# Attention beside a gelu MLP on one core: which side work may go on in a step of the main loop, finer steps, and a chunk's scaling moved ahead

## The chip, the core and the metric

The kernel runs on one core of a Trainium2 chip. The core has five engines that matter here: TensorE (PE in the profile, its weight loads PEld) multiplies matrices into PSUM, VectorE (DVE) and ScalarE (ACT) work element by element, GpSimd (POOL) does a little set-up, and SyncE (SP) issues most DMA transfers. Each engine takes its instructions strictly in the order in which the program lists them and waits where one needs another engine's result. The metric is the device time of one execution in microseconds; the figure given is the median of several executions.

## What is computed

The input has 2048 tokens of width 640. After a layer norm without weights, two branches are added to the input: multi-head attention with 32 heads of width 20, and a second layer norm with a two-layer MLP of width 1536 and tanh-approximated gelu. All arrays are float32.

```python
xn = _layernorm(x, axis=-1)
return x + _A_ref(xn, A_wqkv, A_wo) + _B_ref(xn, B_w1, B_b1, B_w2, B_b2)

# _A_ref: 32 heads of width 20
scores = jnp.einsum("bhqd,bhkd->bhqk", q, k) * (Dh ** -0.5)
p = _softmax(scores, axis=-1)
o = jnp.einsum("bhqk,bhkd->bhqd", p, v)
return o.transpose(0, 2, 1, 3).reshape(B, S, D) @ wo

# _B_ref
y = _layernorm(x, axis=-1)
h = _gelu(jnp.einsum("bsd,df->bsf", y, w1) + b1)
return jnp.einsum("bsf,fd->bsd", h, w2) + b2
```

## The kernel before

**Stages.** From 0 to about 232 us the kernel normalises x, splits the weights into pairs of 16-bit numbers and computes q, k and v; q and k, and the normalised x, go out to DRAM. From 232 to about 1308 us runs the attention loop, into which the MLP is woven. After that only the output projection is left (lines 872 to 904), which runs to 1377 us on TensorE, with the last output store behind it.

**The attention loop.** The heads are taken in 16 pairs `g` and two halves `hf` of the queries (`ORDER`, line 37): the first twelve pairs take both halves in turn, the last four take all first halves and then all second halves. One `(g, hf)` has two column blocks `cc` of 512 queries and 16 blocks `kb` of 128 keys. A *unit* is one `kb` of both heads: two score matmuls into a PSUM tile `s` of which there are three (line 584), and one exponential on ScalarE over 128 x 1024 (line 586). Four units are a *group*; there are 256 groups. For the first two units of each group VectorE computes `low`, what the upper 16 bits of `p` leave (line 598). `pv` (lines 603 to 638) multiplies a group's `p` and `low` with the values into the PSUM tile `o`; it is issued one group late, so that the product of group n follows the scores of group n + 1.

**The order written by hand** stands in lines 933 to 962. For each group it is: scores of units 0 and 1, a `tick()`, `low` of unit 0, a slice of *fill*, scores of units 2 and 3, a `tick()`, `low` of unit 1, and the product of the previous group. So there are two ticks in a group.

**Fill** is the generator `chain()`: the MLP's matmuls, then the output projection. Each group gives it a credit of 1.235 us (`rate`), and its yields book the cost of the matmuls issued: 0.3276 us for three matmuls of the first layer (`pu`, line 787), 0.272 us for two of the second (`py`, line 819), 0.408 us for three of the projection (`z`, line 896). A slice ends when the credit or `CHUNK` is used up, or when a PSUM tile has been completed (`over`). The MLP goes through eight chunks of 256 tokens (`MC`). Within a chunk six first-layer tiles alternate with four second-layer tiles of the chunk before; at the border between two chunks three first-layer tiles follow one another with one second-layer tile among them. There is one PSUM tile `m` (pool `psM`, one buffer) for `pu`, `py` and `z` alike, so a new tile's matmuls wait until VectorE has read the last.

**Side work** is a list of generators, `sides`; every tick takes each of them one step further (lines 520 to 530). They are:

- `gelu` (lines 735 to 753), one for each first-layer tile, begun when its matmuls are done: two vector instructions that read the tile, at the next tick two more, a tick later nothing, then the tanh on ScalarE, then three vector instructions. The first tile of a chunk also scales the chunk's row factors `r2f` (line 739).
- `addup` (lines 755 to 762), one vector instruction for each second-layer tile, and the store and next load of the running sum at the second of two.
- `load_stack` (lines 131 to 152): the DMAs that bring the next pair's q and k.
- `finish` (lines 666 to 733), the heads' normalisation, run one after another by `finishing()`. After pairs 3, 6, 9, 12, 14 and 16 (`ENDS`), for each half, the outputs and the sums of the exponentials come back from DRAM; VectorE adds, checks and inverts the sums (lines 702 to 707, the small group); the inverse goes through DRAM to be spread over rows; then, for each of two column blocks, four vector instructions add, scale and split the outputs (lines 725 to 731, each in a tick of its own), and a DMA stores them to `oscr`. The very last one is timed by the counts `W1` and `W2` in ticks after the loop.
- `prep_late` (lines 534 to 558): once the last chunk's first layer is done, wo is loaded into the room of w1, its squares are summed on ScalarE (line 541), a matmul adds the sums over partitions (line 110), and VectorE splits wo (lines 552 to 557).

The chunk's x and row factors are loaded by `load_chunk` (lines 769 to 775) about one chunk ahead. `projection()` starts a piece only when its heads are finished (`known`, line 873).

Of the kernel before, what the change touches and what calls it, by code (L numbers as in the profile page):

```python
# [12 lines left out]
ALU = mybir.AluOpType  # L13
# [29 lines left out]
def mha_mlp_kernel(tc, x, wqkv, wo, w1, b1, w2, b2, out):  # L43
# [4 lines left out]
    with (  # L48
# [463 lines left out]
        with ExitStack() as scope:  # L512
# [7 lines left out]
            sides = []  # L520

            def begin(it):

                if next(it, self_end) is not self_end:
                    sides.append(it)

            def tick():
                for it in list(sides):
                    if next(it, self_end) is self_end:
                        sides.remove(it)  # L530

            self_end = object()

            def prep_late(tag, w, wv_, src, nk, slices, delay):
                nc.sync.dma_start(w, src)
                for _ in range(delay):
                    yield
                acc = sm.tile([P, 8], F32, tag="acc", name="acc")
                for i, sl in enumerate(slices):
                    junk = m1.tile([P, 2 * MC], F32, tag="u", name="junk").bitcast(BF16)[:, :D]  # L540
                    nc.scalar.activation(junk, w[:, sl, :], AF.Square, accum_out=acc[:, i : i + 1])
                    yield
                pw[tag] = pow2(acc[:, : len(slices)], tag)
                s = keep.tile([P, 1], F32, name=f"s_{tag}")
                nc.vector.tensor_scalar(s, pw[tag][1], 4096.0, None, ALU.mult)
                nc.vector.tensor_scalar(fo, pw["v"][0], 2.0**-22, pw[tag][0], ALU.mult, ALU.mult)
                yield
                for k in range(nk):
                    parts = []
                    for tag_, c0 in (("u", 0), ("w", 320)):  # L550
                        tmp = m1.tile([P, 2 * MC], F32, tag=tag_, name="wtmp")[:, :320]
                        nc.vector.tensor_scalar(tmp, w[:, k, c0 : c0 + 320], s, None, ALU.mult)
                        parts.append((tmp, slice(c0, c0 + 320)))
                    yield
                    for tmp, cols in parts:
                        nc.vector.tensor_copy(wv_[:, k, 0, cols], tmp)
                        nc.vector.tensor_sub(wv_[:, k, 1, cols], tmp, wv_[:, k, 0, cols])
                    yield
# [85 lines left out]
            def unload(g, hf, ev):  # L644
                cols = slice(hf * 1024, (hf + 1) * 1024)
                for p in range(2):
                    dma(g, hf)(lpart[p, hf, 2 * g : 2 * g + 2, :].rearrange("a (c t) -> a c t", c=2),
                                      ev[PAD + DH + VW * p :: 64])
                    for a in range(2):
                        q0, r = 64 * a + PAD + VW * p, (2 * g + a) * DH  # L650
                        dma(g, hf)(opart[p, r : r + DH, cols].rearrange("d (c t) -> d c t", c=2),
                                          ev[q0 : q0 + DH])
                if g + 1 in ENDS:
                    fins.append(finish(g + 1 - UNITS[ENDS.index(g + 1)], g + 1, hf))
                    if len(fins) == 1:
                        sides.append(finishing())
# [9 lines left out]
            def finish(g0, g1, hf):  # L666
# [9 lines left out]
                for c0 in range(0, 1024, w):  # L676
# [21 lines left out]
                    if c0 == 0:  # L698
                        for _ in range(W1 if last else 4):
# [5 lines left out]
                                                accum_out=good[: nh * 16, n : n + 1])  # L705
                        nc.vector.tensor_scalar(l[:, 0], l[:, 0], 1e-30, None, ALU.max)
# [28 lines left out]
            def gelu(ps, r2f, hT, f):  # L735
                u = m1.tile([P, 2, MC], F32, tag="u", name="u")
                w = m1.tile([P, 2, MC], F32, tag="w", name="w")
                if f == 0:
                    nc.vector.tensor_scalar(r2f, r2f, f1, None, ALU.mult)
                nc.vector.tensor_mul(u, ps, r2f[:, None, :].to_broadcast([P, 2, MC]))  # L740
                nc.vector.tensor_add(u, u, b1t[:, f : f + 2, None].to_broadcast([P, 2, MC]))  # L741
                yield
# [3 lines left out]
                yield  # L746
# [6 lines left out]
                                               ALU.mult, ALU.subtract)  # L753

            def addup(ps, xb, t0, hf):
                cols = slice(hf * 320, (hf + 1) * 320)
                nc.vector.scalar_tensor_tensor(xb[:, cols], ps[:, :320], f2, xb[:, cols], ALU.mult, ALU.add)  # L757
                if hf == 1:
                    yield
                    nc.sync.dma_start(accscr[t0 : t0 + P, :], xb)  # L760
                    if t0 + P < S:
                        load_xb(t0 + P)
# [3 lines left out]
            xs, hTs = {}, {}  # L766
            over = [False]

            def load_chunk(mc):
# [5 lines left out]
                xs[mc] = xnt, r2f  # L775

# [95 lines left out]
            def projection():  # L872
                known = lambda c: ready[2 * c // NMC] == len(UNITS)
# [53 lines left out]
            with tc.manual_schedule():  # L927
# [4 lines left out]
                prev = None  # L932
                for g, hf, cc, kb0 in groups:
                    units = []
                    for kb in range(kb0, kb0 + GRP):
# [4 lines left out]
                        if kb % GRP == 1:  # L940
# [5 lines left out]
                            spent, over[0] = 0.0, False  # L946
                            while credit > 0 and spent < CHUNK and not over[0]:
                                cost = next(fill)
                                if cost is None:
                                    credit = 0.0  # L950
                                    break
                                credit -= cost
                                spent += cost
                        else:
                            for u in units[1:]:
                                rest(u)
                            if prev:
                                pv(prev)
                    prev = units
# [21 lines left out]
                while sides:  # L981
                    tick()
# [100 lines left out]
```

## Time and profile before

| what | us |
|---|---|
| median of 3 executions (1384.6 to 1388.05) | 1384.71 |
| the profiled execution, its own time | 1385.2 |
| the profiled execution, span from first to last instruction | 1383.5 |
| attention loop, first exponential to last | 233.2 to 1306.5 |
| 1024 exponentials on ScalarE, busy | 973.6 |
| 512 `low` on VectorE, busy | 608.8 |
| ScalarE idle before exponentials, waiting for scores | 46.2 |
| VectorE idle before `low`, waiting for exponentials | 164.9 |

The page of the profile has the busy time of each engine, the chain of work that ended last, and groups of instructions by source line. A stretch of time can be cut out and its busy times shown; the list of waits names, for each instruction that found its engine idle, what ended the idle time; the timeline shows instructions in order of time, merged where equal ones follow one another. The kernel's lines carry the numbers printed above; L598 is line 598. A matmul's end is modelled, so a busy TensorE need not be one at its best speed.

### The profile page before, as it was taken

Reading aid. Unit: us, or ns where it says so; the run is one execution under the profiler, and the core shown is the slowest. Engines: PE = TensorE matmul, PEld = TensorE weight load, DVE = VectorE, ACT = ScalarE, POOL = GpSimd, SP = SyncE. Lnnn points to the kernel's source line nnn. Section 1 sums busy time; section 2 is a strip of 40 time slices with the busy share of each in tenths; the row PEclk is TensorE's granted clock in tenths of the full one; section 3 lists DMA queues with packets and bytes.
Section 4 is the critical chain, followed back from the end, with each engine's and each line's share of the span. In section 5 each row is a group of like instructions: output and inputs, shape, how many; then the busy total and the mean of one; then the engine's idle time right before and its main releaser. Section 6 shows DMA issues by size and latency. Waiting matters only on the chain.

```text
span 1383.5 us, 29113 instructions
## 1 busy us (share of the span) xinstructions
PE 1350.8 (98%) x11711; PEld 600.9 (43%) x11711; DVE 1061.7 (77%) x1425; ACT 1126.2 (81%) x1282; POOL 32.9 (2%) x75
## 2 busy tenths in 40 slices
PE   9999999999999999999999999999999999999998
PEld 6555555443333343433343333343334334333375
DVE  6648743899778977889887789877988897888642
ACT  5644323999999999999999999999999999999700
POOL 2000000000000000000000000000000000000000
PEclk9999999999999999999999999999999999999999
DMA  9853413012124231213221123212124322341375
GB/s 265 243 175 109 108 52 110 16 32 64 41 55 111 67 88 34 69 52 102 71 77 33 47 75 103 76 47 58 44 64 113 98 56 70 85 153 59 98 235 179
DMA packets 92320, 125.68 MB, mean 91 GB/s; under 512 B 16905, under 2 KB 58569, under 8 KB 92178
## 3 DMA queue, kind: packets, MB, share of 16 engines
q1 hardware_dynamic: 89218, 117.14, 28.3%
q0 software_dynamic: 2304, 5.24, 2.3%
q8 instruction: 94, 1.54, 0.5%
q10 hardware_dynamic: 656, 1.36, 0.3%
q14 instruction: 48, 0.39, 0.1%
HBM read 80.84 MB, written 42.86 MB: 89 GB/s over the span
## 4 chain that ended last, share of the span: by engine, by line
PE 59%; DVE 11%; ACT 5%; DMA 3%; issue 2%; SPq 1%; DVEq 0%; ACTq 0%
PE o L615 23%; PE s L584 14%; PE py L819 9%; PE pu L787 8%; DVE low L598 5%; PE z L896 5%; ACT p L586 4%; DMA oscr<-oa 1%; DVE u L740 1%; DMA oa<-opart 1%; DVE u L741 1%; DVE w L744 1%; DVE w L745 1%; DVE hT L752 1%; DVE u L750 1%
## 5 line engine op out<-in xcount | busy, mean ns | idle before, releaser
L586 ACT ACTIVATE p<-s 128x1024 f32<-128x1024 f32 x1024 | 973.6, 1042 | 52.4 <-PE s L584 46.2
L598 DVE TENSOR_TENSOR low<-p 128x1024 f16<-128x1024 f32 x512 | 608.8, 1219 | 165.0 <-ACT p L586 164.9
L615 PE MATMUL o<-p,vfull 128*32 128x512 bf16 (+1 forms) x4096 | 433.7, 494 | 0.0
L584 PE MATMUL s<-qs,ks 61*128 61x512 f16 x2048 | 317.7, 382 | 8.7 <-ACT p L586 7.2
L584 PEld LDWEIGHTS <-ks 61*128 61x128 f16 x2048 | 63.9, 94 | 296.4 <-issue 294.2
L787 PE MATMUL pu<-xm,w1t 128*128 128x256 f16 x1440 | 179.2, 274 | 4.1 <-DVE u L740 3.6
L819 PE MATMUL py<-w2t,hT 128*128 128x320 f16 x1152 | 178.6, 301 | 1.7 <-DVE xb L757 1.7
L787 PEld LDWEIGHTS <-w1t 128*128 128x128 f16 x1440 | 130.9, 98 | 71.2 <-issue 57.6
L819 PEld LDWEIGHTS <-hT 128*128 128x128 f16 x1152 | 102.5, 98 | 89.5 <-issue 55.2
L286 PE MATMUL qkp<-xnt,wv 128*128 128x512 f16 x600 | 132.3, 380 | 0.0
L615 PEld LDWEIGHTS <-vfull 128*32 128x32 f16 x3072 | 61.5, 95 | 146.2 <-issue 115.4
L615 PE MATMUL o<-low,vfull 128*32 128x512 f16 x1024 | 107.3, 379 | 6.6 <-DVE low L598 6.4
L300 ACT ACTIVATE qkhl<-qkp,qks 128x1024 f16<-128x1024 f32 (+1 forms) x24 | 23.3, 971 | 84.1 <-PE qkp L286 66.2
L286 PEld LDWEIGHTS <-wv 128*128 128x128 f16 x600 | 58.2, 98 | 67.8
L615 PEld LDWEIGHTS o<-p,vfull 128*32 128x32 f32 x2048 | 63.1, 109 | 50.6 <-issue 0.5
L349 PE MATMUL vp<-wv,xnt 128*128 128x320 f16 x480 | 66.6, 300 | 0.0
L896 PE MATMUL z<-w1t,ot 128*128 128x320 f16 x480 | 65.8, 300 | 0.0
L896 PEld LDWEIGHTS <-ot 128*128 128x128 f16 x480 | 46.7, 98 | 19.8 <-issue 1.7
L349 PEld LDWEIGHTS <-xnt 128*128 128x128 f16 x480 | 46.5, 98 | 18.2
L301 DVE SCALAR_TENSOR_TENSOR qkhl<-qkp,qks,qkhl 128x1024 f16<-128x1024 f32 (+1 forms) x24 | 26.5, 1104 | 34.3 <-ACT qkhl L300 34.3
L857 DVE SCALAR_TENSOR_TENSOR acc<-z,sc,acc 128x320 f32<-128x320 f32 x32 | 17.6, 550 | 45.1 <-PE z L896 42.9
L636 ACT ACTIVATE ev<-o 128x512 f32<-128x512 f32 x64 | 39.4, 615 | 3.3 <-PE o L615 3.3
(168 smaller groups left out, 685.7 us busy)
## 6 DMA issues: line engine op xcount, KB each, us to landing
qkscr<-qkhl SPq DMA_DIRECT2D x40, 256.0 KB
opart<-ev SPq DMA_DIRECT2D x124, 80.0 KB
ks<-qkscr SPq DMA_DIRECT2D x120, 80.0 KB
qs<-qkscr SPq DMA_DIRECT2D x192, 40.0 KB
oa<-opart SPq DMA_DIRECT2D x32, 240.0 KB
xt<-in_A_x_dram SPq DMA_DIRECT2D x16, 320.0 KB
xscr<-xnt SPq DMA_DIRECT2D x4, 1280.0 KB
xm<-xscr SPq DMA_DIRECT2D x8, 640.0 KB
```

The costliest lines, as they stand in the source:

```text
L286: nc.tensor.matmul(ps[:, i, :], wv[:, k, q, a, mm * P : (mm + 1) * P], xnts[c][:, k, b, :], start=(k + n == 0), stop=(k == KD - 1 and n == 2))
L300: nc.scalar.activation(hl[:, 0, i0:i1], ps[:, i0:i1], AF.Copy, scale=a)
L301: nc.vector.scalar_tensor_tensor(hl[:, 1, i0:i1], ps[:, i0:i1], a, hl[:, 0, i0:i1], ALU.mult, ALU.subtract)
L349: nc.tensor.matmul(ps[:, hf, :320], xnts[c][:, k, a, j * P : (j + 1) * P], wv[:, k, 2, b, hf * 320 : (hf + 1) * 320], start=(n == 0), stop ...
L584: nc.tensor.matmul(ps[:, a, :], ks[64 * a : 64 * a + 61, kb * P : (kb + 1) * P], qs[64 * a : 64 * a + 61, cc * 512 : (cc + 1) * 512], star ...
L586: nc.scalar.activation(pt, ps, AF.Exp, scale=QS)
L598: nc.vector.tensor_sub(low, pt, upper(pt))
L615: nc.tensor.matmul(pv.o[32 * q : 32 * q + 32, :], src[:, v0 - PAD * (1 - q % 2) :][:, :32], t, start=q not in pv.begun, stop=last, skip_gr ...
L636: nc.scalar.activation(evs[g, hf][:, cc], pv.o, AF.Copy)
L787: nc.tensor.matmul(ps[:, i], w1v[:, k, (f + i) // 4, a, fo_ : fo_ + P], xnt[:, k, b, :], start=(n == 0), stop=(n == 3 * KD - 1))
L819: nc.tensor.matmul(ps[:, :320], hTs[mc][:, f, a, j * P : (j + 1) * P], w2v[:, f, b, hf * 320 : (hf + 1) * 320], start=(n == 0), stop=(n == ...
L896: nc.tensor.matmul(ps[:, :320], ot[:, k, a, j * P : (j + 1) * P], wov[:, k, b, h * 320 : (h + 1) * 320], start=(n == 0), stop=(n == 3 * KD ...
```

## The change

`tick()` now keeps two lists. Work in `sides` goes on at every tick; each step may yield the VectorE time, in us, that it has just issued. Work in `patient` goes on only in a tick in which neither the sides nor a generator begun since the last tick booked any. All finishings are patient except those of second halves from pair 12 on. `prep_late` waits two ticks more ahead of its matmul, and splits its casts into two steps; the projection now also waits for the end of that split. The small group of a finishing is in two steps. The scaling of `r2f` is done by a patient generator eight ticks after the chunk's load, for chunks from the third on, and otherwise where it was. In the very first group, which has no product to issue, a second slice of fill stands in the product's place.

```diff
+            sides, patient = [], []
+            taken = [0.0]
 
             def begin(it):
-                if next(it, self_end) is not self_end:
+                t = next(it, self_end)
+                if t is not self_end:
                     sides.append(it)
+                    taken[0] += t or 0.0
 
             def tick():
-                for it in list(sides):
-                    if next(it, self_end) is self_end:
-                        sides.remove(it)
+                t, taken[0] = taken[0], 0.0
+                for its in (sides, patient):
+                    if its is patient and t > 0:
+                        break
+                    for it in list(its):
+                        r = next(it, self_end)
+                        if r is self_end:
+                            its.remove(it)
+                        else:
+                            t += r or 0.0
...
             def prep_late(tag, w, wv_, src, nk, slices, delay):
...
                     yield
+                yield
+                yield
                 pw[tag] = pow2(acc[:, : len(slices)], tag)
...
-                yield
+                yield 1.0
                 for k in range(nk):
...
-                    yield
+                    yield 0.6
                     for tmp, cols in parts:
                         nc.vector.tensor_copy(wv_[:, k, 0, cols], tmp)
                         nc.vector.tensor_sub(wv_[:, k, 1, cols], tmp, wv_[:, k, 0, cols])
-                    yield
+                        yield 0.7
+                split_done.append(tag)
...
                     if len(fins) == 1:
-                        sides.append(finishing())
+                        (sides if hf == 1 and g + 1 >= TAIL else patient).append(finishing())
...
                         nc.vector.tensor_scalar(l[:, 1], l[:, 0], LO, None, ALU.is_ge, ALU.min,
                                                 accum_out=good[: nh * 16, n : n + 1])
+                        if not last:
+                            yield
                         nc.vector.tensor_scalar(l[:, 0], l[:, 0], 1e-30, None, ALU.max)
...
             def gelu(ps, r2f, hT, f):
-                if f == 0:
-                    nc.vector.tensor_scalar(r2f, r2f, f1, None, ALU.mult)
+                scale_rows(r2f)
                 nc.vector.tensor_mul(u, ps, r2f[:, None, :].to_broadcast([P, 2, MC]))
                 nc.vector.tensor_add(u, u, b1t[:, f : f + 2, None].to_broadcast([P, 2, MC]))
-                yield
+                yield 1.2
 
                 nc.vector.tensor_mul(w, u, u)
                 nc.vector.scalar_tensor_tensor(w, w, 1.0 / 0.044715, u, ALU.add, ALU.mult)
-                yield
+                yield 1.2
...
+                yield 1.7
+
+            def scale_rows(r2f):
+                if r2f in unscaled:
+                    unscaled.remove(r2f)
+                    nc.vector.tensor_scalar(r2f, r2f, f1, None, ALU.mult)
+
+            def scale_ahead(r2f):
+                for _ in range(8):
+                    yield
+                scale_rows(r2f)
 
             def addup(ps, xb, t0, hf):
...
-                if hf == 1:
-                    yield
+                if hf == 0:
+                    yield 0.5
+                else:
+                    yield 0.5
...
             def load_chunk(mc):
...
                 xs[mc] = xnt, r2f
+                unscaled.append(r2f)
+                if mc > 1:
+                    patient.append(scale_ahead(r2f))
...
-                known = lambda c: ready[2 * c // NMC] == len(UNITS)
+                known = lambda c: split_done and ready[2 * c // NMC] == len(UNITS)
...
+                def other():
+                    nonlocal credit
+                    spent, over[0] = 0.0, False
+                    while credit > 0 and spent < CHUNK and not over[0]:
+                        cost = next(fill)
+                        if cost is None:
+                            credit = 0.0
+                            break
+                        credit -= cost
+                        spent += cost
...
                             credit += rate
-                            spent, over[0] = 0.0, False
-                            while credit > 0 and spent < CHUNK and not over[0]:
-                                cost = next(fill)
-                                if cost is None:
-                                    credit = 0.0
-                                    break
-                                credit -= cost
-                                spent += cost
+                            other()
                         else:
                             for u in units[1:]:
                                 rest(u)
                             if prev:
                                 pv(prev)
+                            else:
+                                credit += rate
+                                other()
...
-                while sides:
+                while sides or patient:
                     tick()
```

## The prediction

> **What bounds the kernel now.** I read the page first, then busy time by stretches, then who waited for whom, then the instructions in order of time where TensorE stood still.
>
> ```profile
> span 1383.5 us, 29113 instructions
> PE 1350.8 (98%) x11711; PEld 600.9 (43%) x11711; DVE 1061.7 (77%) x1425; ACT 1126.2 (81%) x1282; POOL 32.9 (2%) x75
> L586 ACT ACTIVATE p<-s x1024: 1011/1028/1197, 233.2 to 1306.5; 128x1024 f32<-128x1024 f32 x171
> ```
>
> TensorE is busy 98% of the span; the kernel can only win where TensorE waits or is held up. The third row (the exponentials by source line: shortest/median/longest ns, first and last start) gives the attention loop: 1024 exponentials, four to a group, so 256 groups from 233.2 to about 1308. I cut it where every eighth group starts its first exponential; six of the 32 stretches (columns: length, then busy us of PE, PEld, DVE, ACT, POOL, clock, DMA):
>
> ```profile
> 736.30:768.70 32.40, 32.40 (x304) 12.71 (x302) 24.33 (x25) 31.57 (x36) 0.00 (x0) 1.00 0.13 35
> 434.70:471.70 37.00, 33.71 (x312) 13.70 (x310) 33.03 (x44) 32.83 (x38) 0.85 (x1) 1.00 0.37 99
> 834.40:870.80 36.40, 33.65 (x312) 13.79 (x310) 34.70 (x47) 32.52 (x38) 0.00 (x0) 1.00 0.33 96
> 702.10:736.30 34.20, 33.30 (x313) 13.76 (x311) 31.78 (x38) 32.48 (x38) 0.00 (x0) 1.00 0.16 43
> 1235.80:1271.20 35.40, 33.41 (x300) 12.70 (x298) 28.47 (x49) 34.72 (x45) 0.00 (x0) 1.00 0.34 105
> 1271.20:1308.00 36.80, 33.98 (x304) 12.91 (x306) 31.00 (x44) 31.35 (x35) 2.39 (x3) 1.00 0.23 66
> ```
>
> The first is a clean one: TensorE never idles and eight groups take 32.4 us. ScalarE is close behind at 31.57. The 32.4 hold 9.8 us of fill (the MLP matmuls, 1.235 us booked a group), so a group without fill takes (32.4 - 9.8) / 8 = 2.83 us of TensorE. Against 32.5, the others lose 4.5, 3.9, 1.7, 2.9 and 4.3 us. In the second and third VectorE is the busy one: a finishing of heads falls on the border of two MLP chunks there, where three gelu tiles follow each other closely. The fourth is such a border with no finishing. The last two hold the late preparation of wo.
>
> ```profile
> PE s L584 <- ACT p L586: 7.2, 24, 0.5
> PE o L615 <- DVE low L598: 6.4, 11, 1.5
> PE pu L787 <- DVE u L740: 3.6, 4, 2.0
> PE py L819 <- DVE xb L757: 1.7, 2, 1.3
> PE mxp L110 <- ACT junk L541: 1.2, 1, 1.2
> ```
>
> TensorE's direct waits on VectorE in the loop are 11.7 us (6.4 + 3.6 + 1.7); the change can only reach these, their after-effects, and the 1.2 on ScalarE. What such a wait looks like:
>
> ```profile
> 448.10 1.22 DVE L598 TENSOR_TENSOR low<-p 128x1024 f16<-128x1024 f32 x1
> 449.24 0.68 DVE L731 TENSOR_TENSOR oa<-oa 120x512 f16<-120x512 f32 x1
> 449.84 0.68 DVE L750 SCALAR_TENSOR_TENSOR u<-w,u 128x512 f32<-128x512 f32 x1
> 451.75 1.22 DVE L598 TENSOR_TENSOR low<-p 128x1024 f16<-128x1024 f32 x1
> 452.89 0.35 DVE L739 TENSOR_SCALAR r2f<-r2f,sc 128x256 f32<-128x256 f32 x1
> 453.34 0.69 DVE L740 TENSOR_TENSOR u<-pu,r2f 128x512 f32<-128x512 f32 x1
> 456.12 1.22 DVE L598 TENSOR_TENSOR low<-p 128x1024 f16<-128x1024 f32 x1
> 454.08 1.47 PE L787 MATMUL pu<-xm,w1t 128*128 128x256 f16 x12 [1.99 <-DVE u L740]
> ```
>
> Line 740 empties the only psM buffer, and the next tile's matmuls wait 1.99 us for it. VectorE has no gap: the last finishing step (731), the second half of a gelu, a low and the chunk's scaling (739) stand ahead. From start to start, these rows give VectorE's prices: low 1.14 us, step 731 0.60, second gelu half 449.84 to 451.75 = 1.91, scaling 0.45, first gelu half 453.34 to 456.12 = 2.78.
>
> **The change, part by part.** The program holds the same instructions on every engine (1639 vector ones in both), so nothing is saved outright; only their places move. So I set VectorE's demand against TensorE's over runs of four to eight groups, in each kernel's own order. Example, groups 49 to 52 of before: 8 lows (9.1), two first halves (5.6), two second (3.8), four finishing steps (0.61 + 0.60 + 0.33 + 0.60 = 2.1), one scaling (0.45): 21.1 us, against 4 x 2.84 + 4.9 fill = 16.3 for TensorE, an excess of 4.8. Over six groups there it is 5.8 (loss 4.5), in the third stretch 5.4 (loss 3.9), in the fourth 2.9 (loss 1.7). So about 0.7 us is lost per us of the largest excess; I use 0.7, with 0.5 and 1.0 as ends.
>
> 1. *Finishing steps held.* A step goes on only in a tick whose other work booked no VectorE time. A gelu has two ticks of that kind in its middle, so in the new order the steps stand right behind the first halves, not away from the border. At the first border the excess falls from 5.8 to 4.1, at the second from 5.4 to 3.8: gains of 1.2 and 1.1. But at the border near 702 to 736, now free, the held steps of the heads that ended 60 us earlier arrive: all four stand among three gelus, and 2.9 becomes 4.6, a loss of 1.2. A fourth (1086 to 1153) keeps its 3.1 to 3.3.
> 2. *Small group in two steps.* These took 1.2 us in one go, between the halves of a gelu:
>
> ```profile
> 861.21 0.21 DVE L702 TENSOR_TENSOR lt<-lt 96x64 f32<-96x64 f32 x1
> 862.41 0.62 DVE L744 TENSOR_TENSOR w<-u 128x512 f32<-128x512 f32 x1
> 864.95 0.40 PE L615 MATMUL o<-low,vfull 128*32 128x512 f16 x3 [1.51 <-DVE low L598]
> ```
>
>    Behind them TensorE waited 1.51 us for a low. In the new order they stand elsewhere, in two ticks. Part of this is in the excess above; I add half, 0.75 (ends 0 and 1.5).
> 3. *Factors scaled ahead.* Six of eight scalings (0.45 each) leave the front of a border's first gelu. Where a finishing meets the border it is counted above; at the two other borders the excess falls by 0.45, 0.3 us each: 0.6 in all (ends 0 and 0.9). The cover is VectorE's idle quarter (24.33 of 32.40 in the clean stretch); without it the 0.45 would be back.
> 4. *Late preparation of wo.* Five squares on ScalarE, then the matmul of their sums:
>
> ```profile
> 1247.93 0.84 ACT L541 ACTIVATE junk<-w1t 128x640 bf16<-128x640 f32 x1
> 1259.07 0.39 PE L110 MATMUL mxp<-acc,ones 128*128 128x5 f32 x2 [1.24 <-ACT junk L541]
> 1272.68 1.79 PE L819 MATMUL py<-w2t,hT 128*128 128x320 f16 x12 [1.29 <-DVE xb L757]
> ```
>
>    Two more ticks (about 4 us) lie between the last square and that matmul: the wait of 1.24 goes (ends 0.2, if ScalarE's backlog merely shows up at the next scores, and 1.24). Splitting one step into two spreads the casts: largest excess from 4.8 to 3.3, gain 1.05 (ends 0.5 and 2.8, the whole of the waits for xb and of the clump). The squares themselves stay. The new gate on the projection (split_done) costs nothing: in the new order the last cast stands in group 252 and the first projection matmul in group 255.
> 5. *One more fill slot, in group 0.*
>
> ```profile
> 237.01 0.82 PE L787 MATMUL pu<-xm,w1t 128*128 128x256 f16 x6 [0.54 <-DMA xm<-xscr]
> 233.00:236.00 3.00, 1.25 (x8) 0.29 (x6) 1.77 (x2) 3.00 (x5) 0.00 (x0) 1.00 0.69 202
> 239.00:242.00 3.00, 3.00 (x24) 0.64 (x16) 1.25 (x2) 1.63 (x3) 0.00 (x0) 0.63 0.70 195
> ```
>
>    TensorE has room in group 0 (1.25 busy of 3.00), but the slot's six matmuls need xm, which lands at 237.0 as before. They move ahead of two score pairs and wait there; all fill then runs one group earlier, and 12 projection matmuls come into the loop. Earlier fill bought by an equal delay: 0.2 us lost (ends -1.0 and +1.5). Behind the slot wait the scores, and for those ScalarE, about 1 us idle, which the border after it can absorb.
>
>    The Trainium skill (TensorE: Matmul & The Clock Gate, section What's actually happening) says an idle window of some 3.4 us halves the array's clock until it is busy again. The trace agrees: behind the thin 233 to 236 the granted clock is 0.63. By that rule a second such window could come at this place, an estimate of 1.7 us more; the sum doesn't use it.
> 6. *The tail.*
>
> ```profile
> 1324.31 45.81 PE L896 MATMUL z<-w1t,ot 128*128 128x320 f16 x336
> 1335.54 0.38 ACTq L732 DMA_DIRECT2D oscr<-oa  x1
> 1339.27 0.96 SPq L851 DMA_DIRECT2D ot<-oscr  x2
> ```
>
>    Tail matmuls take 45.81 / 336 = 0.136 us; 12 fewer save 1.6. But the last heads' store (1335.54) is timed by ticks from the loop's end, the fifth piece's load (1339.27) follows its landing on SyncE's queue behind two output stores, and the piece's matmuls now come due 1.6 earlier, at about 1342.3 instead of 1343.9, three us after the issue. I take 1.2 as lost again; with 12 more matmuls in the loop (about 0.9, part of the fill above) the net is +0.6 (ends -1.2 and +1.4).
>
> Sum: -1.2 - 1.1 + 1.2 - 0.1 - 0.75 - 0.6 - 1.24 - 1.05 + 0.2 + 0.6 = -4.0 us. The profiled execution took 1385.2 of its own, so 1381.2; the median of the runs lies 0.5 below it, hence 1380.7.
>
> **Rivals.** *All overlaps clear (faster).* The losses at the two bad borders fall to the 1.7 of a border without finishing (-2.8 and -2.2), the fourth likewise (-0.4), the third isn't hurt, the end loses only its squares (-4): 9.4, so 1375.3. For it: the listed waits of 1.99, 1.51 and 1.29 each have a moved instruction just ahead. Against: the new order still puts finishing steps into three borders.
>
> *The change doesn't do what it says.* A gelu's quiet ticks count as free though VectorE is still behind, so the excess is only carried to other groups; borders gain and lose alike, and only the 1.24 on mxp goes, less 0.8 from parts 5 and 6: 1384.3. For it: the same 1639 instructions, and the third border. The Trainium skill (VectorE: DVE Perf Modes, section The DRAIN you can't avoid) holds that each vector operation waits for the pipe to empty, so only fewer operations help, which speaks for this one; the start-to-start prices above agree that nothing overlaps by more than about 0.1 us.
>
> *The psM turn-around takes over (slower).*
>
> ```profile
> 455.49 0.61 PE L584 MATMUL s<-qs,ks 61*128 61x512 f16 x4
> 666.55 1.64 PE o L615 x19
> 1086.10:1153.30 67.20, 66.28 (x618) 26.90 (x616) 60.59 (x76) 63.77 (x72) 0.86 (x1) 1.00 0.29 80
> ```
>
> From a tile's last matmul to the next tile's first lie two blocks of scores and one product, 0.61 + 1.64 + 0.61 = 2.9 us. Where VectorE is further behind than that when line 740 comes up, TensorE stops. (The third row is the stretch of sixteen groups around the fourth border: 16 x 2.84 plus 19.6 of fill are 65.1, so 2.1 lost.) Now that happens badly at two borders; steps packed behind first halves could make it happen at all four, each at the worst loss measured, 4.5: 18.0 instead of 4.5 + 3.9 + 1.7 + 2.1 = 12.2, so +5.8, less 1.24, plus 0.8: 1390. Against: at two of the four the excess falls.
>
> **How the numbers follow.** Likeliest, 0.58: 1380.7, own range 1377 to 1384. All clear 0.18 (1375.3), no effect 0.14 (1384.3), slower 0.10 (1390). A measurement of this kernel tells about 0.3%, 4.2 us, from no change: below 1380.5 is faster, above 1388.9 slower. The likeliest case sits on that bound, half (0.29) to each side; with 0.17 of the second case faster is 0.46. Slower: 0.09. Same: the other halves and no effect, 0.45. Range 1375 to 1386.
>
> **What would show it.** Right: no wait of pu for u above 1 us near 452; the 1.51 and the 1.24 gone; the two bad stretches near 35 us and a worse one than 34.2 near 702 to 736. Part 5: pu first in group 0, waiting about 2 us for xm. Part 6: a gap of about 1 us ahead of the fifth piece. Wrong: bad stretches below 34 (all clear), or waits for u at all four borders (slower).

## The result, and the profile after

The changed kernel takes 1377.07 us (median of 6 runs, 1375.98 to 1382.35) against 1385.78 (6 runs, 1384.6 to 1388.05; the 1384.71 that the forecast starts from is the median of the first three of these) for the kernel before on the same chip: ratio 0.9942, 95% interval 0.9931 to 0.9953, about 8 us faster. The forecast of 1380.7 had the direction and its range held the time, but the gain is twice the 4.0 us of the sum. The profiled execution took 1378.13 us of its own, its span is 1376.4.

First the page of the changed kernel, span and busy time by engine:

```profile
span 1376.4 us, 29091 instructions
PE 1347.3 (98%) x11711; PEld 599.3 (44%) x11711; DVE 1061.0 (77%) x1425; ACT 1125.5 (82%) x1282; POOL 32.6 (2%) x75
```

TensorE is busy 3.5 us less than before, VectorE and ScalarE within 1 us, with as many instructions on each (1425 on VectorE in both profiles; the prediction's 1639 is not a count of the profile). So no work went; the places changed. In the code the lines have moved: the exponential is now L602, low L614, the product L631, the first finishing step L744, the emptying of psM L758, pu L823, py L855, z L932.

Who waited for whom on TensorE in the changed kernel (us in total, times, longest; rows of the stages ahead of the loop left out):

```profile
PE s L600 <- ACT p L602: 5.5, 18, 0.6
PE o L631 <- DVE low L614: 3.7, 7, 0.8
PE pu L823 <- DMA xm<-xscr: 2.7, 1, 2.7
PE pu L823 <- DVE u L758: 1.1, 3, 0.5
PE py L855 <- DVE u L758: 1.1, 2, 0.8
PE z L932 <- DMA ot<-oscr: 0.8, 1, 0.8
PE py L855 <- DVE xb L787: 0.7, 1, 0.7
PE z L932 <- DVE acc L893: 0.6, 1, 0.6
PE mxp L110 <- ACT p L602: 0.2, 1, 0.2
```

The waits on VectorE fall from 11.7 us to 6.6 (3.7 + 1.1 + 1.1 + 0.7), none longer than 0.8: the 1.99 and the 1.51 are gone, and the 1.24 of mxp is 0.2. The wait for xm has grown from 0.5 to 2.7, and the two of z, behind the loop, are new. The eight-group stretches that hold the first bad border, the border that had been free, and the second bad one, in the order of time (length, busy PE, PEld, DVE, ACT, POOL, clock, DMA):

```profile
436.80:471.32 34.52, 33.29 (x311) 13.53 (x309) 33.11 (x42) 32.53 (x37) 0.00 (x0) 1.00 0.23 70
701.69:736.92 35.23, 33.35 (x312) 13.61 (x310) 34.33 (x42) 32.58 (x37) 0.00 (x0) 1.00 0.26 75
834.70:869.94 35.24, 33.92 (x314) 13.81 (x312) 34.77 (x44) 32.74 (x38) 0.00 (x0) 1.00 0.21 60
```

They took 37.0, 34.2 and 36.4 before. The two bad ones are near 35 and the one that was free is worse by 1: what the forecast named. At the first of them, by time:

```profile
448.03 1.22 DVE L614 TENSOR_TENSOR low<-p 128x1024 f16<-128x1024 f32 x1
449.17 0.68 DVE L758 TENSOR_TENSOR u<-pu,r2f 128x512 f32<-128x512 f32 x1
449.91 1.47 PE L823 MATMUL pu<-xm,w1t 128*128 128x256 f16 x12 [0.52 <-DVE u L758]
```

Neither a scaling nor a finishing step stands between the low and the line that empties psM; the wait of 1.99 is 0.52.

For the whole loop I cut at each group's first exponential and call *loss* of a stretch what its length has over 2.84 us a group and over the fill issued in it (0.109 us for a pu matmul, a third of the 0.3276 that the kernel books for three, beside 0.108 from the 12 in 1.47 and the 6 in 0.82 that the prediction shows; 0.136 for one of py or z). Worked out from the two traces:

```
groups     0-4  4-44 44-56 56-108 108-122 122-140 140-172 172-236 236-256   sum
before     2.4   5.4   4.3    2.4     1.4     0.4     4.4     5.5     7.2   33.4
after      4.8   3.4   2.2    2.4     2.3     0.4     2.0     2.8     3.5   24.0
forecast  +0.2     0  -1.2      0    +1.2       0    -1.1    -0.1    -2.3   (and -1.35 for parts 2 and 3, not placed)
```

The loss falls by 9.4, twelve projection matmuls more take 1.6 of it, and the loop goes from 1074.4 to 1066.6 us. Ahead of the loop lie 233.2 and 233.4 us, behind it 76.0 and 76.4. A second profile of the same kernel (e1_again) repeats every stretch behind group 4 to 0.03 us; in groups 0 to 3 it has 3.7 and not 4.8. So the stretches tell more than the total times, which for this kernel spread over 3 us in one set of runs (e1_again) and over 6 in the other.

What differs in groups 0 to 3 is the granted clock (the last column but two): before, the changed kernel, the changed kernel again, and the kernel before with the holding alone (e8_hold_only):

```profile
233.18:249.93 16.75, 14.49 (x119) 5.27 (x118) 9.45 (x8) 15.09 (x18) 0.00 (x0) 0.90 0.41 110
```
```profile
233.43:252.89 19.46, 15.96 (x123) 5.97 (x123) 9.53 (x10) 15.05 (x17) 0.00 (x0) 0.82 0.33 95
```
```profile
232.78:251.09 18.31, 14.97 (x123) 5.71 (x123) 9.53 (x10) 15.05 (x17) 0.00 (x0) 0.91 0.37 101
```
```profile
232.12:250.15 18.03, 15.67 (x119) 5.40 (x118) 9.44 (x8) 15.26 (x17) 0.00 (x0) 0.81 0.36 102
```

Over all profiles here it is either 0.90 to 0.91 or 0.81 to 0.83, with the slot and without it. Without the slot these groups lose 2.4 to 2.7 at the higher clock and 3.6 to 3.7 at the lower; with it 3.5 to 3.7 and 4.8 to 5.0. So the slot costs about 1.1 us at the start, and the lower clock, which comes to either kernel, as much again. Kernels are best compared by what they lose behind the first four groups: 31.0 before, 19.2 in both profiles of the changed kernel.

The start and the tail of the changed kernel:

```profile
237.57 1.44 PE L823 MATMUL pu<-xm,w1t 128*128 128x256 f16 x6 [2.68 <-DMA xm<-xscr]
239.59 1.94 ACT L602 ACTIVATE p<-s 128x1024 f32<-128x1024 f32 x2 [2.39 <-PE s L600]
...
1337.02 25.98 PE L932 MATMUL z<-w1t,ot 128*128 128x320 f16 x190 [0.76 <-DMA ot<-oscr]
```

The slot waits 2.68 us for xm, the scores stand behind it and ScalarE idles 2.39. In the tail the fifth piece waits 0.76 for its load, near the 1 us forecast.

### The profile page after: what moved, and what is told of

It is laid out like the page before. It is cut to its first block, busy times and chain, and to the rows that moved or that the text cites. A ratio compares the mean times of both kernels' runs of the same rounds, so it can differ in the third digit from the quotient of the medians.

```text
span 1376.4 us, 29091 instructions
## 1 busy us (share of the span) xinstructions
PE 1347.3 (98%) x11711; PEld 599.3 (44%) x11711; DVE 1061.0 (77%) x1425; ACT 1125.5 (82%) x1282; POOL 32.6 (2%) x75
## 4 chain that ended last, share of the span: by engine, by line
PE 66%; DVE 8%; ACT 3%; DMA 2%; issue 2%; SPq 1%; DVEq 0%; ACTq 0%
PE o L631 26%; PE s L600 16%; PE py L855 11%; PE pu L823 9%; PE z L932 4%; DVE low L614 3%; ACT p L602 3%; DVE u L758 1%; DVE u L759 1%; DVE w L762 1%; DMA oscr<-oa 1%; DMA acc<-accscr 0%; DVE w L763 0%; DVE hT L770 0%; DVE u L768 0%
## 5 line engine op out<-in xcount | busy, mean ns | idle before, releaser
L602 ACT ACTIVATE p<-s 128x1024 f32<-128x1024 f32 x1024 | 973.9, 1043 | 46.2 <-PE s L600 38.9
L614 DVE TENSOR_TENSOR low<-p 128x1024 f16<-128x1024 f32 x512 | 610.6, 1218 | 162.4 <-ACT p L602 161.7
L631 PE MATMUL o<-p,vfull 128*32 128x512 bf16 (+1 forms) x4096 | 430.2, 493 | 0.0
L823 PE MATMUL pu<-xm,w1t 128*128 128x256 f16 x1440 | 181.1, 275 | 3.8 <-DMA xm<-xscr 2.7
L855 PE MATMUL py<-w2t,hT 128*128 128x320 f16 x1152 | 178.6, 300 | 1.7 <-DVE u L758 1.1
L823 PEld LDWEIGHTS <-w1t 128*128 128x128 f16 x1440 | 131.5, 98 | 72.1 <-issue 57.8
L855 PEld LDWEIGHTS <-hT 128*128 128x128 f16 x1152 | 102.5, 98 | 89.3 <-issue 55.1
L631 PEld LDWEIGHTS <-vfull 128*32 128x32 f16 x3072 | 60.4, 95 | 137.7 <-issue 106.3
L631 PE MATMUL o<-low,vfull 128*32 128x512 f16 x1024 | 103.5, 378 | 3.7 <-DVE low L614 3.7
L631 PEld LDWEIGHTS o<-p,vfull 128*32 128x32 f32 x2048 | 62.1, 108 | 52.3
L932 PE MATMUL z<-w1t,ot 128*128 128x320 f16 x480 | 66.3, 299 | 1.4 <-DMA ot<-oscr 0.8
L932 PEld LDWEIGHTS <-ot 128*128 128x128 f16 x480 | 46.5, 98 | 21.9 <-issue 2.9
```

The lines of the kernel that those rows point to most:

```text
L602: nc.scalar.activation(pt, ps, AF.Exp, scale=QS)
L614: nc.vector.tensor_sub(low, pt, upper(pt))
L631: nc.tensor.matmul(pv.o[32 * q : 32 * q + 32, :], src[:, v0 - PAD * (1 - q % 2) :][:, :32], t, start=q not in pv.begun, stop=last, skip_gr ...
L823: nc.tensor.matmul(ps[:, i], w1v[:, k, (f + i) // 4, a, fo_ : fo_ + P], xnt[:, k, b, :], start=(n == 0), stop=(n == 3 * KD - 1))
L855: nc.tensor.matmul(ps[:, :320], hTs[mc][:, f, a, j * P : (j + 1) * P], w2v[:, f, b, hf * 320 : (hf + 1) * 320], start=(n == 0), stop=(n == ...
L932: nc.tensor.matmul(ps[:, :320], ot[:, k, a, j * P : (j + 1) * P], wov[:, k, b, h * 320 : (h + 1) * 320], start=(n == 0), stop=(n == 3 * KD ...
```

## The experiments

Each edit is to the changed kernel unless it says that it is to the kernel before. All times are medians, ratios to the kernel before on the same chip.

**e1_again: the changed kernel, unaltered.**

> The changed kernel once more, unaltered, as the yardstick on the chip of the next three. All theories: 0.994 of the kernel before, 8 us faster.

Measured 1378.41, ratio 0.9943 (0.9931 to 0.9955).

**e2_no_hold: no step is held.**

```
-  (sides if hf == 1 and g + 1 >= TAIL else patient).append(finishing())
+  sides.append(finishing())
```

> The changed kernel, but every finishing goes on at every tick (none is patient); all else stays. Demand theory (what counts is VectorE's largest excess over TensorE at a chunk border, 0.7 us lost for each us): the excesses at the four borders with a finishing are 4.6, 2.5, 4.7 and 2.2 in this order against 4.1, 4.6, 3.8 and 3.1 with holding, sum 14.0 against 15.6, so about 1 us faster than the changed kernel. Holding theory (steps kept out of booked ticks are what pays): most of the 4.7 us that the four borders and the stretches behind them gained comes back, 3 to 5 us slower than the changed kernel.

Measured 1382.47, ratio 0.9976 (0.9964 to 0.9988): 4 us of the 8 are gone; the excess of VectorE's demand alone had said 1 us *faster*. VectorE's own waits in e2_no_hold show what is late:

```profile
DVE oa L744 <- DMA oa<-opart: 5.9, 3, 3.2
DVE oa L744 <- DMA qs<-qkscr: 1.3, 1, 1.3
```

The second row names a load that this step does not read, so what it waited for there is open. By time, around the longest of the waits (other rows between these left out):

```profile
640.10 0.79 SPq L714 DMA_DIRECT2D oa<-opart  x2
...
646.37 0.69 DVE L744 TENSOR_TENSOR oa<-oa 120x512 f32<-120x512 f32 x1 [3.22 <-DMA oa<-opart]
646.97 1.22 DVE L614 TENSOR_TENSOR low<-p 128x1024 f16<-128x1024 f32 x1
648.11 0.68 DVE L758 TENSOR_TENSOR u<-pu,r2f 128x512 f32<-128x512 f32 x1
648.84 2.06 PE L855 MATMUL py<-w2t,hT 128*128 128x320 f16 x14 [1.53 <-DVE u L758]
651.33 1.94 ACT L602 ACTIVATE p<-s 128x1024 f32<-128x1024 f32 x2 [2.06 <-PE s L600]
```

The loads of oa are issued at 640.10, and the first finishing step can start at 646.37. VectorE works in order, so the low and the emptying of psM stand behind it, TensorE waits 1.53 for those, and ScalarE 2.06 for TensorE. The changed kernel has no VectorE wait for oa or rb at all. From here there are two theories: *demand* (what counts is where the steps' VectorE time lies, as in the prediction) and *landing* (what counts is whether the loads have landed when the first step comes up).

**e3_no_slot: no slot in group 0.**

```
-  else:
-      credit += rate
-      other()
```

> The changed kernel without the extra slice of fill in group 0. Theory from the profile after (the slice stands 2.7 us before the landing of xm and holds up two score blocks): groups 0 to 3 lose 2.4 us rather than 4.8, and the 0.6 us wait for acc right behind the loop goes, so 2.5 to 3.5 us faster than the changed kernel. Rival (the slice is worth its fill, 12 projection matmuls of 0.136 us less in the tail): 1.6 us slower.

Measured 1388.49, ratio 1.0018 (1.0003 to 1.0034): 10 us above e1_again on the same chip, and neither side had that. (The profiled execution took 1384.47, the fastest of its 12.) Groups 64 to 72 lose 5.1 in it and -0.1 in the changed kernel, by one event:

```profile
514.35 2.26 SPq L740 DMA_DIRECT2D rb<-linv  x6
...
518.40 0.69 DVE L744 TENSOR_TENSOR oa<-oa 120x512 f32<-120x512 f32 x1 [5.16 <-DMA rb<-linv]
...
520.88 3.20 PE L855 MATMUL py<-w2t,hT 128*128 128x320 f16 x12 [3.26 <-DVE u L758]
...
524.73 1.94 ACT L602 ACTIVATE p<-s 128x1024 f32<-128x1024 f32 x2 [5.34 <-PE s L600]
```

The same chain, longer. It isn't the slot itself: without it all fill comes a group later, and here a step comes up before its load has landed. Groups 4 to 44 and 236 to 256 lose 2.0 and 2.9 more besides.

**e4_old_prep: the preparation of wo as it was before** (casts in one step, no two ticks ahead of the sums).

> The changed kernel with the late preparation of wo as before (no two ticks ahead of the matmul, casts in one step). The stretch from group 243 on gained 3.9 us. Preparation theory: all of it is this part, 3.5 to 4 us slower than the changed kernel. Demand theory: excess 5.1 instead of 3.3, times 0.7, and the 1.24 wait on the squares' sum: 2.5 us slower. Rival (shifted phase, not this part): within 1 us.

Measured 1380.03, ratio 0.9957 (0.9945 to 0.9969). Only the stretch 236 to 256 moves, 3.5 to 5.8, and the old wait is back among TensorE's:

```profile
PE mxp L110 <- ACT junk L554: 1.2, 1, 1.2
```

So part 4 is worth 2.3 us in the loop (1.6 by the medians of the same chip, 1380.03 and 1378.41); the sum had 1.24 + 1.05.

**e5_no_hold_long: e2_no_hold with more time between the loads and the first step.**

```
-  for _ in range(W2 if last else 4):
+  for _ in range(W2 if last else 8):
```

> The changed kernel with the finishing steps not held (as in e2_no_hold, 1382.5), but with eight ticks instead of four between the loads of the heads' partial outputs (oa, rb) and the first finishing step. Landing theory (holding paid because the first finishing step no longer stands on VectorE waiting for its DMA, 5.9 us of such waits in e2_no_hold and none in the changed kernel): VectorE's waits for oa and rb fall below 1 us and about 4 us come back, 1377.5 to 1380. Demand theory (holding paid by where the steps' VectorE time lies; the excesses of this order sum to 0.6 us more than in e2_no_hold): no recovery, 1382 to 1384.

Measured 1377.51, ratio 0.9946 (0.9926 to 0.9966); VectorE waits for neither oa nor rb. The whole loss of e2_no_hold comes back without any holding. But the four ticks also move the steps, so this alone doesn't part the theories.

**e6_no_slot_long: e3_no_slot with seven ticks there.**

> The changed kernel without the slot of fill in group 0 (as in e3_no_slot, 1388.5), but with seven ticks instead of four between the loads and the first finishing step. Landing theory: the single event of 5.6 us near group 68, where the first finishing step waited 5.16 us for rb, goes, and with it most of the other 2.6 us of waits for oa: 1381 to 1384. Slot theory (the slot itself is worth 10 us, because all fill runs a group earlier): it stays at 1387 to 1390.

Measured 1421.92, ratio 1.026 (1.0238 to 1.0282), far outside of both. The loop did what landing says: it takes 1066.3 us (1074.7 in e3_no_slot), groups 56 to 92 lose 1.4 (6.4), and behind the first four groups it loses 21.8 (30.2; 19.2 in the changed kernel). But the time behind the loop went from 76 to 120 us. TensorE's and VectorE's waits:

```profile
PE z L932 <- DMA ot<-oscr: 31.6, 7, 18.3
```
```profile
DVE oa L744 <- DMA oa<-opart: 15.7, 2, 10.1
DVE lt L719 <- DMA lt<-lpart: 12.7, 1, 12.7
```

The finishings stand in one queue, each step held until VectorE is unbooked. With seven ticks a finishing takes so long that the queue hasn't emptied when the loop ends: its last held first step stands in group 254, the others run behind the loop, and the projection waits 31.6 us for their results. That is the price of holding when the queue runs late; neither theory had it, and the prediction had it among no rival.

**e7_before_long: the kernel before, eight ticks there.**

> The kernel before with one edit, eight ticks instead of four between the loads and the first finishing step. Landing theory: its 2.7 us of VectorE waits for oa and rb go, and with them about 2 us, 1383 to 1385 beside 1386 for the kernel before, ratio 0.997 to 0.9995. Demand theory (excesses of this order 0.2 above those of before): 1386, ratio 1.000.

Measured 1383.67, ratio 0.9983 (0.9974 to 0.9992), 2.4 us by the ratio, as landing had it. e12_before_early shows that this reading was wrong. By stretch the border 44 to 56 gains 1.8, 108 to 122 loses 2.0, and 236 to 256 gains 2.0.

**e8_hold_only: the kernel before with the holding alone.**

> The kernel before with the holding alone (and the bookings of VectorE time that it needs). Landing theory: the held steps come later, so VectorE's waits for oa and rb (2.7 us in before) go, about 2 us, and the steps also leave two borders: 1382 to 1385. Demand theory as predicted (-1.2 -1.1 +1.2 -0.1): 1385. If the gain of the changed kernel is all in the holding: 1379.

Measured 1382.59, ratio 0.9973 (0.9961 to 0.9986). By stretch against before: 44 to 56 from 4.3 to 2.4, 140 to 156 from 3.6 to 2.0, 108 to 122 from 1.4 to 2.6. The sum falls from 33.4 to 31.0 with the lower clock at the start in this profile; behind the first four groups from 31.0 to 27.3, by 3.7, as the ratio says. The forecast had -1.2, -1.1, +1.2 for these borders: the signs are right, the two gains larger (-1.9, -1.6), the loss met.

**e9_early_load: e2_no_hold with its loads issued earlier.** The halves of a finished result are written over rb, so the next load of oa needn't wait until their store has landed. VectorE's instructions and their order are those of e2_no_hold.

```
-  hl = o1.bitcast(F16)...
+  hl = (o1 if last else rb).bitcast(F16)...
```

> The changed kernel without the holding (as in e2_no_hold, 1382.5), but the two halves of a finished result are written over rb and no longer over oa, so that the next loads of oa need not wait for the store to land. VectorE's instructions are those of e2_no_hold, in the same order; only the loads are issued some 2.8 us earlier. Landing theory: VectorE's waits for oa fall from 5.9 us to below 2.5, and 2 to 4 us come back: 1378.5 to 1380.5, the loss in groups 92 to 108 falls from 2.6 to below 1. Demand theory: the order decides, so 1382 to 1383 and 2.6 there as before.

Measured 1377.47, ratio 0.9932 (0.9919 to 0.9945): 5 us better than e2_no_hold (on another chip; behind the first four groups the loss is 3.8 less), as fast as the changed kernel. The same place as above (other rows left out):

```profile
637.43 0.37 SPq L751 DMA_DIRECT2D oscr<-rb  x1
637.85 0.90 SPq L714 DMA_DIRECT2D oa<-opart  x2
...
643.54 0.68 DVE L744 TENSOR_TENSOR oa<-oa 120x512 f32<-120x512 f32 x1
646.34 0.68 DVE L758 TENSOR_TENSOR u<-pu,r2f 128x512 f32<-128x512 f32 x1
647.72 2.08 PE L855 MATMUL py<-w2t,hT 128*128 128x320 f16 x14
650.22 1.95 ACT L602 ACTIVATE p<-s 128x1024 f32<-128x1024 f32 x2 [0.47 <-PE s L600]
```

The loads of oa follow the store (L751) by 0.42 us; in e2_no_hold it was issued at 636.88 and they at 640.10, 3.2 later. No wait ahead of the first step, none of TensorE. Groups 92 to 108, first e2_no_hold, then e9_early_load:

```profile
619.19:687.10 67.91, 65.96 (x608) 25.75 (x606) 58.39 (x73) 63.45 (x72) 0.87 (x1) 1.00 0.27 75
```
```profile
619.67:685.56 65.89, 65.89 (x608) 25.68 (x606) 58.49 (x73) 63.45 (x71) 0.87 (x1) 1.00 0.29 79
```

The same work, 2.0 us less, all of it TensorE's idle time; groups 188 to 204 give the other 1.6. With VectorE's order fixed, demand can't tell these two apart: inside the changed kernel the holding pays because its steps come after their loads. Demand isn't wrong, though: with no step waiting, the four borders of e9_early_load lose 0.2 more, 1.0 less, 0.7 more and 0.6 less than those of the changed kernel, and 0.7 times the excesses in the expectation of e2_no_hold gives +0.35, -1.5, +0.6 and -0.6.

**e10_no_split_scale: without parts 2 and 3.**

```
-  if not last:
-      yield
...
-  if mc > 1:
-      patient.append(scale_ahead(r2f))
```

> The changed kernel without its parts 2 and 3: the small group is again in one step, and a chunk's factors are scaled by the first gelu that needs them. As predicted they are worth 0.75 + 0.6 = 1.35 us: 1378.9 to 1380 beside 1377.5 to 1378.4 for the changed kernel. If the holding alone carries all: no difference, 1377 to 1378.4. Landing theory adds that one tick less between the group's sums and the store of linv brings the first finishing step one tick nearer to its loads: up to 2 us more, 1381 to 1382, with VectorE waits for rb or oa back in the profile.

Measured 1382.76, ratio 0.9971 (0.9959 to 0.9982). The loss rises at five chunk borders by 0.4, 0.3, 0.5, 0.5 and 0.5 (44-56, 80-92, 108-122, 172-188, 204-220), 2.2 in all, and by 2.4 between 56 and 80; the sixth border whose scaling moved, 140 to 156, stays. Between 56 and 80 VectorE waits at the first finishing step (L742 here), where the changed kernel doesn't:

```profile
DVE oa L742 <- DMA oa<-opart: 3.5, 1, 3.5
```

Of the three expectations landing's, 1381 to 1382, comes nearest.

**e11_credit_only: the slot is credited in group 0, and spent in group 1.**

```
   else:
       credit += rate
-      other()
```

> The changed kernel with the slot of group 0 only credited, not spent there: its six matmuls of the MLP come in group 1 instead, behind the landing of xm. As predicted the slot made TensorE wait 2 us for xm with two score pairs behind it; the changed kernel's profile shows 2.7, and a loss in groups 0 to 3 of 3.7 to 4.8 against 2.4 before. If that wait is a loss: 1 to 2.4 us faster than the changed kernel, 1375.3 to 1377. If the loop absorbs it, or the order after it takes a worse phase: 1377 to 1379.

Measured 1375.8, ratio 0.9920 (0.9906 to 0.9934), the fastest kernel here. TensorE's wait for xm is 1.0 instead of 2.7, groups 0 to 3 lose 3.3 at a granted clock of 0.90 (3.5 to 3.7 with the slot at 0.91), and all later stretches are those of the changed kernel. The loop says 0.2 to 0.4 us; the medians, taken on different chips, say 1.3 to 2.6, and the intervals of the ratios just overlap. So the slot's place costs a little in the loop; no trace shows the rest.

**e12_before_early: the kernel before with the edit of e9_early_load.**

> The kernel before with the one edit of e9_early_load: the halves of a finished result go over rb and not over oa. VectorE's order is that of the kernel before; the loads are issued earlier. In before the first finishing step waits for oa or rb in groups 59 (1.22 us) and 155 (1.00), both behind a chunk border. If landing is what e7_before_long gained by (3.0 us): 1383 to 1384.5, and the loss in groups 44 to 56 falls from 4.3 towards 2.5. If the order of the steps at the border is what costs there, and the two waits fall where VectorE had room: the waits go, but groups 44 to 56 keep 4.3, and the time is 1385 to 1386.8.

Measured 1385.29, ratio 0.9995 (0.9982 to 1.0008). VectorE's waits for oa and rb are gone, but the first border is still bad. TensorE's waits for the emptying of psM are those of before, 3.6 in all and 2.0 at the longest (1.9 and 1.0 in e8_hold_only, with 0.9 more ahead of py):

```profile
PE pu L787 <- DVE u L740: 3.6, 4, 2.0
```

Its stretch 44 to 56:

```profile
418.95:471.78 52.83, 49.79 (x464) 20.22 (x463) 48.07 (x62) 48.14 (x55) 0.85 (x1) 1.00 0.34 94
```

It loses 3.8 (4.3 before, 2.5 in e7_before_long). Behind the first four groups the loss is 30.0 instead of 31.0. In the kernel before, landing is worth about 1 us by the stretches (0.7 by the ratio, whose interval reaches 2.5); what e7 and e8 gained at the borders came in the main from where the steps lie, as the prediction said.

## Why the prediction was half right

*The mechanism of part 1 was right for the kernel it was read from, and its size is the term furthest off.* The steps left two borders and came to a third (e8, e12). But the holding alone takes 3.7 from the loss behind the first four groups, not 1.2. The two bad borders gain 3.5 instead of 2.3, and the rest comes from stretches where the sum had nothing: 92 to 108 (0.5), and 56 to 80 and 156 to 172 (0.2 and 0.6, which e12 shows to be landing).

*Parts 2 and 3* were too small as well: 2.2 instead of 1.35, without the 2.4 that landing adds between 56 and 80. At the two borders with no finishing the scaling was priced right (e10: 0.3 and 0.5, forecast 0.3 each). At three of the four others its removal cost 0.5 each, near one for one for an instruction of 0.45, and at the fourth nothing. The wait of 1.51 that part 2 was read from is gone with the holding alone (e8: no wait for a low above 0.8), so what the split does of itself, beyond giving a load one more tick, is not shown.

*Part 4* was right in mechanism and size (2.3 measured, 2.29 in the sum).

*Part 5 came out near the sum, but not by its reason.* "Earlier fill bought by an equal delay: 0.2 us lost" put the loss at the start. There it is about 1.1 at an equal granted clock, with a wait of 2.7 for the 2 forecast. What failed is the step from there to the rest of the loop: groups 4 to 44 lose 3.3 to 3.4 in every kernel whose fill runs a group earlier (e11 too, without the slot's matmuls), and 5.3 to 5.4 in every one where it doesn't (before, e3, e6, e7, e8, e12). That is 2.0 us in a stretch which the sum held at nothing: 0.9 of shorter time (167.4 instead of 168.3 us) and the rest more fill. With the 1.1 it makes -0.9, just inside the part's own range from -1.0, and by luck: neither term was foreseen in its size. Why one group earlier suits these groups better, no run took apart.

By the rule on the clock that the prediction named (the Trainium skill, TensorE: Matmul & The Clock Gate, section What's actually happening), a second slow window could come at the start, an estimate of 1.7 us more. The trace shows such a window: the clock not granted over groups 0 to 3 is 0.18 of 19.46 us, 3.5, in the first profile of the changed kernel, and 0.09 of 18.31, 1.6, in the second. But e8_hold_only, which has no slot, shows it too (0.19 of 18.03, 3.4), so it is not the slot that makes it.

*Part 6* had the cause right and the size too small. (Its terms add to +0.5, not +0.6.) It took 1.2 of the 1.6 us that twelve matmuls save behind the loop as lost again, so 0.4 less there; measured are 0.4 to 0.5 more (76.4 and 76.5 beside 76.0). To the wait of 0.76 for the fifth piece's load comes one of 0.64 for acc behind the first piece, which the kernel before doesn't have and the sum had not.

*What the sum lacked* is the landing of the loads. It is little of the difference between before and after (e12), so it isn't what the forecast missed; but it decides what each part is worth beside the others: the holding 4 us, the split and scaling 2.4 of their 4.6, the slot 5.2 of its 10. Behind the first four groups the loss falls by 11.8. As far as runs show, that is the holding (3.7), the preparation (2.3), the scaling and split (2.2) and groups 4 to 44 (2.0), 10.2 together. The 1.6 left is a balance: groups 236 to 256 gain 1.9 and 188 to 204 gain 0.9 beyond these parts, 56 to 92 lose 1.3; these are not taken apart here. Against the 11.8 stand 2.4 at the start, 1.6 for the twelve matmuls, 0.4 behind the loop and 0.2 ahead of it, which leaves the 7.1 between the two spans.

*The rivals.* "All overlaps clear" (1375.3) came nearer to the measured time than the forecast did, but not by its own reason: the border stretches still lose 2.2, 2.3 and 2.3 (44 to 56, 108 to 122, 140 to 156), and the one that had been free, 108 to 122, was hurt, as the forecast had it. "The change doesn't do what it says" fell: the same 1425 vector instructions, 8 us less. The prediction had set beside it that each vector operation waits for the pipe to empty (the Trainium skill, VectorE: DVE Perf Modes, section The DRAIN you can't avoid). VectorE's own busy time did stay (1061.7 and 1061.0 us); that only fewer operations help doesn't hold for the time of the kernel. The slower rival fell: the worst wait for u is 0.8.

## What to carry to other kernels

In these runs an instruction of VectorE that waited for a DMA held up what stood behind it, and through that TensorE and ScalarE. So before a step that needs a DMA is placed on it, compare the time from the load's issue to the step with the time the load took, in each kernel by its own view of that engine's waits, not only TensorE's. Where VectorE was behind, an instruction of 0.45 us moved away was worth 0.3 to 0.5 at five borders of six. A stretch at the start whose granted clock changes from execution to execution is best left out when kernels are compared by their traces. Work that is held for a quiet moment needs a bound: one that keeps its queue from running past the loop whose result it feeds.

## What the runs showed of the hardware

In e2_no_hold the two loads of oa (240 KB each in the list of DMA issues) issued from 640.10 let their reader start at 646.37, 6.3 us later, while loads and stores of the same SyncE queue were issued around it; where the step came up sooner VectorE stood for up to 5.16 us, TensorE behind it for 3.26, and ScalarE behind TensorE for 5.34 (e3_no_slot). Two executions of the changed kernel agree to 0.03 us in every stretch behind the first four groups; they differ in the time ahead of the loop (233.4 and 232.8) and in groups 0 to 3 (4.8 and 3.7). In all fourteen profiles the granted clock over groups 0 to 3 is 0.90 to 0.91 (eight) or 0.81 to 0.83 (six), in kernels with and without the slot, and the lower one goes with 0.9 to 1.5 us more loss there.
